# A decode kernel's five instruction streams, emitted into the program itself instead of into a Block

## Chip, cores and metric

One core of a Trainium2 chip. The metric is the device time of one execution in microseconds (us), as a median over runs; lower is better. A profile also gives the span: from the first to the last recorded instruction of the core. Measured time and span are different things.

## The reference

One decode step of a transformer layer. A normalized token `xn` goes through grouped-query attention over a cache of 65,536 positions (4 key/value heads, 32 query heads, head size 128) and, in parallel, through a small MLP mixer; both are added to `x`.

```python
def reference(A_x, A_k_cache, A_v_cache, A_wq, A_wo, B_x, B_w1, B_w2, B_w3, B_w4):
    # _A_ref: q = x @ wq; softmax(q k^T / sqrt(Dh)) v over the cache; @ wo     (cut)
    # _B_ref: layernorm, w1, gelu, shifted groups, w2, layernorm, w3, gelu, w4  (cut)
    x = A_x
    xn = _layernorm(x, axis=-1)
    return x + _A_ref(xn, A_k_cache, A_v_cache, A_wq, A_wo) + _B_ref(xn, B_w1, B_w2, B_w3, B_w4)
```

The output is one row of 1024 bfloat16 values. The caches and weights are about 170 MB, all read once.

## The kernel before

Each engine has a queue object that records waits, operations and DMAs; dependencies become waits until a semaphore, a counter that engines and DMAs raise, has reached a constant. At the end the recorded lists are emitted, one per engine, into a `Block`. A Block gives each engine a body of its own to branch to, and behind the bodies it places a meeting of all five engines, called the rendezvous here: nobody leaves until all have arrived.

```python
class _Q:
    def emit(self, eng):
        for o in self.ops:
            if o[0] == 0:
                eng.wait_ge(o[1], o[2])          # wait on a semaphore
            elif o[0] == 1:
                ins = o[1](eng)
                if o[2]:
                    ins.then_inc(self.sem, 1)
            else:
                o[1](eng).then_inc(o[2], 16)     # DMA

    with ExitStack() as es:
        E = es.enter_context
        block = E(nc.Block())                    # entered first, so left last
        # ... (cut: tiles, semaphores, the whole computation recorded into q_pe, q_dve, q_act, q_pool, q_sp)
        for i in range(len(w4_parts)):
            w4_pe(i)                             # the last matmuls, into OUT_ps
        _op(q_dve, lambda e: e.tensor_copy(orow[:, :], OUT_ps[:, 0:256]), reads=[b_OUT], writes=[b_orow])
        ev_out = _dma(q_sp, chan("out"), lambda e: e.dma_start(out=out[0, 0, :].rearrange("(j n) -> j n", j=4), in_=orow[0:97:32, :]), reads=[b_orow])
        q_sp.wait(ev_out)                        # SyncE waits until the store has landed

        block.sync(lambda e: q_sp.emit(e))
        block.tensor(lambda e: q_pe.emit(e))
        block.vector(lambda e: q_dve.emit(e))
        block.scalar(lambda e: q_act.emit(e))
        block.gpsimd(lambda e: q_pool.emit(e))
```

## Time and profile before

| | before |
|---|---|
| measured time, median of 3 runs | 403.76 us (403.68 to 404.6) |
| span in the profile | 401.93 us |
| measured time of the profiled run | 403.64 us |
| last weights land | 398.93 us |
| store issued, store landed | 399.87, 401.53 us |

A DMA lands when the last update of its semaphore is recorded. "The landing" below is that of the output's store.

The page of the kernel before says what bounds it. The lines are its span, the busy time of each engine, the load queue (packets, MB, share of the 16 DMA engines' time) and the chain that ended last, by engine.

```profile
span 401.9 us, 5169 instructions
...
PE 193.7 (48%) x2059; PEld 83.0 (21%) x2059; DVE 227.8 (57%) x400; ACT 48.3 (12%) x127; POOL 61.8 (15%) x90
...
q1 hardware_dynamic: 6920, 169.87, 98.4%
...
DMA 54%; DVE 22%; PE 17%; ACT 3%; issue 2%; SPq 0%; POOL 0%; ACTq 0%
...
```

No compute engine is near its limit, and one queue keeps the DMA engines 98.4% occupied: the kernel moves its bytes as fast as the DMA engines do. The view by windows (busy time with the number of instructions for each engine, then the TensorE clock, the DMA share and GB/s) shows where this holds and where it ends:

```profile
...
core 0: us, PE busy (x) PEld busy (x) DVE busy (x) ACT busy (x) POOL busy (x), PEclk, DMA share, GB/s
...
20.00:100.00 80.00, 34.26 (x472) 15.21 (x469) 45.77 (x92) 9.13 (x22) 8.71 (x10) 1.00 1.00 431
...
300.00:380.00 80.00, 38.83 (x324) 12.34 (x328) 55.87 (x90) 12.51 (x34) 14.40 (x16) 0.61 1.00 430
380.00:399.00 19.00, 11.05 (x194) 6.12 (x190) 1.50 (x5) 0.60 (x1) 1.09 (x1) 0.68 0.88 373
399.00:402.00 3.00, 0.36 (x8) 0.08 (x8) 0.42 (x1) 0.00 (x0) 0.00 (x0) 1.00 0.00 1
...
```

From 20 to 380 us the DMA share is 1.00. In the last three microseconds it is 0.00: the loads are over, and the kernel's own steps there follow one another: last matmuls, cast, store, end. A step removed from that sequence should shorten the kernel by its length. The end of the timeline (start, duration, engine, line, operation; a "q" behind the engine marks its sequencer) shows the sequence:

```profile
...
399.42 0.42 DVE L619 CAST orow<-OUT_ps 128x256 bf16<-128x256 f32 x1 [13.16 <-PE OUT_ps L392]
399.87 0.65 SPq L620 DMA_DIRECT2D out_dram<-orow  x1
```

After the cast and the issue of the store there is no further work, yet the span goes on to 401.93 us. The view of SyncE's waits and the view of the line that opens the Block (engine, operation, count; durations in ns; first and last start in us) show why:

```profile
...
engine line waited for: us in total, times, longest us
...
SPq L155 <- DMA out_dram<-orow: 1.0, 1, 1.0
...
SPq L155 <- PEq L155: 0.2, 1, 0.2
```

```profile
...
L155 POOLq EVENT_SEMAPHORE  x2: 17/17/17, 401.7 to 401.8; - x2
L155 ACTq DRAIN  x1: 627/627/627, 381.2 to 381.2; - x1
L155 POOLq DRAIN  x1: 1197/1197/1197, 381.8 to 381.8; - x1
L155 PEldq DRAIN  x1: 435/435/435, 399.0 to 399.0; - x1
L155 DVEq DRAIN  x1: 464/464/464, 399.4 to 399.4; - x1
L155 SPq COMPARE_BRANCH  x1: 33/33/33, 401.6 to 401.6; - x1
L155 SPq DRAIN  x1: 7/7/7, 401.7 to 401.7; - x1
L155 SPq EVENT_SEMAPHORE  x1: 17/17/17, 401.9 to 401.9; - x1
L155 ACTq EVENT_SEMAPHORE  x1: 17/17/17, 401.9 to 401.9; - x1
L155 DVEq EVENT_SEMAPHORE  x1: 21/21/21, 401.9 to 401.9; - x1
L155 PEldq EVENT_SEMAPHORE  x1: 51/51/51, 401.9 to 401.9; - x1
...
```

SyncE waits 1.0 us for the store, in its branch (the branch instruction carries the wait), and then 0.2 us in the rendezvous. Everything of L155 that starts at 401.6 us or later stands behind the landing of the store. The drains (the DRAIN instructions that the Block puts behind each stream) of the other four engines are over by 399.90 us.

### The profile page before, as it was taken

The page shows a single profiled execution, that of the slowest core. Times are in us where ns is not written, and L with a number is a line of the kernel's source. Part 1 is how long each engine was busy: PE and PEld are TensorE (multiplying, and loading weights), DVE is VectorE, ACT ScalarE, POOL GpSimd, SP SyncE. Part 2 cuts the span into 40 slices and gives each one's busy share as a digit, 9 for nine tenths or more (in the row PEclk, how much of TensorE's full clock was granted, in tenths as well). Part 3 has the DMA queues.
Part 4 walks back from the last instruction along what each step waited for, and adds up shares of the span by engine and source line. Part 5 has one row for each costly group of instructions (what it writes and reads, how often), then busy time and mean ns, then how long its engine had stood idle before and what let it go on. Part 6 is the DMA issues. An engine that isn't in the chain of part 4 may idle for free.

```text
span 401.9 us, 5169 instructions
## 1 busy us (share of the span) xinstructions
PE 193.7 (48%) x2059; PEld 83.0 (21%) x2059; DVE 227.8 (57%) x400; ACT 48.3 (12%) x127; POOL 61.8 (15%) x90
## 2 busy tenths in 40 slices
PE   0361446064525756286640965454443645445645
PEld 0250111021103511062110731121111311111232
DVE  0217666277816588255753388576836775788410
ACT  0000201012101011011110011111201111111200
POOL 5000013011211011110310102111110112112110
PEclk9999999999955565555565556565565855665686
DMA  8999999999999999999999999999999999999994
GB/s 356 427 416 436 444 421 419 450 432 421 444 434 423 432 434 439 416 434 452 423 420 450 426 424 444 432 421 435 430 435 427 445 430 424 424 431 430 436 419 205
DMA packets 7088, 170.20 MB, mean 423 GB/s; under 512 B 916, under 2 KB 920, under 8 KB 1048
## 3 DMA queue, kind: packets, MB, share of 16 engines
q1 hardware_dynamic: 6920, 169.87, 98.4%
q8 instruction: 16, 0.26, 0.2%
q14 instruction: 8, 0.07, 0.0%
q10 hardware_dynamic: 144, 0.00, 0.0%
HBM read 169.87 MB, written 0.00 MB: 423 GB/s over the span
## 4 chain that ended last, share of the span: by engine, by line
DMA 54%; DVE 22%; PE 17%; ACT 3%; issue 2%; SPq 0%; POOL 0%; ACTq 0%
DMA Kn<-in_A_k_cache_dram 43%; DVE X L464 11%; DMA Kn<-in_B_w_dram 6%; DMA Vn<-in_A_wq_dram 5%; PE H_ps L367 4%; DVE pT_f L517 3%; PE S_ps L476 3%; PE OT_ps L524 3%; DVE mrow L483 3%; ACT p_sb L506 3%; PE M_ps L367 2%; PE PT_ps L515 2%; PE M_ps L552 1%; PE OUT_ps L392 1%; DVE Yall L381 1%
## 5 line engine op out<-in xcount | busy, mean ns | idle before, releaser
L464 DVE STREAM_TRANSPOSE X<-Kn 128x1024 f32<-128x1024 f32 x128 | 151.7, 1215 | 64.2 <-DMA Kn<-in_A_k_cache_dram 64.2
L524 PE MATMUL OT_ps<-Vn,pT_f 128*32 128x512 bf16 x512 | 59.9, 620 | 27.2 <-DVE pT_f L517 27.2
L476 PE MATMUL S_ps<-X,Yall 128*32 128x512 bf16 x512 | 57.5, 593 | 17.0 <-DVE X L464 17.0
L489 PE MATMUL MB_ps<-Rm,Lmat 128*128 128x16 bf16 x32 | 6.1, 192 | 87.3 <-DVE Rm L484 87.3
L538 POOL TENSOR_TENSOR O_acc<-O_acc,tmpO 128x513 f32<-128x513 f32 x28 | 32.9, 1174 | 89.0 <-ACT tmpO L532 89.0
L506 ACT ACTIVATE p_sb<-S_ps,brun 128x512 bf16<-128x512 f32 x32 | 22.0, 687 | 172.3 <-DVE brun L504 153.8
L536 POOL TENSOR_SCALAR O_acc<-O_acc,ff 128x513 f32<-128x513 f32 x28 | 19.5, 698 | 149.8 <-ACT ff L511 149.8
L515 PE MATMUL PT_ps<-p_sb,permR 128*128 128x512 bf16 x32 | 18.2, 568 | 39.7 <-ACT p_sb L506 39.7
L483 DVE TENSOR_REDUCE mrow<-S_ps 128x1 f32<-128x512 f32 x32 | 21.6, 674 | 24.2 <-PE S_ps L476 24.2
L532 ACT ACTIVATE tmpO<-OT_ps 128x512 f32<-128x512 f32 x32 | 19.1, 598 | 107.6 <-PE OT_ps L524 107.6
L476 PEld LDWEIGHTS S_ps<-X,Yall 128*32 128x32 bf16 x512 | 16.5, 125 | 54.8 <-DVE X L464 38.6
L517 DVE STREAM_TRANSPOSE pT_f<-PT_ps 128x512 f32<-128x512 f32 x32 | 22.9, 716 | 7.6 <-PE PT_ps L515 7.6
L524 PEld LDWEIGHTS OT_ps<-Vn,pT_f 128*32 128x32 bf16 x512 | 14.5, 127 | 59.2 <-DVE pT_f L517 42.4
L489 PEld LDWEIGHTS MB_ps<-Rm,Lmat 128*128 128x128 bf16 x32 | 3.3, 102 | 111.2 <-DVE Rm L484 111.2
L367 PEld LDWEIGHTS H_ps<-xn_bf,W 128*128 128x128 bf16 x224 | 14.4, 174 | 1.7 <-issue 1.7
L367 PE MATMUL H_ps<-xn_bf,W 128*128 128x1 bf16 x224 | 14.5, 202 | 0.0
L515 PEld LDWEIGHTS PT_ps<-p_sb,permR 128*128 128x128 bf16 x32 | 3.4, 106 | 42.4 <-ACT p_sb L506 42.4
L493 DVE TENSOR_REDUCE Bst<-MB_ps 128x1 f32<-128x16 f32 x32 | 5.6, 174 | 8.3 <-PE MB_ps L489 8.3
L331 PE MATMUL M_ps<-ln_s,ones_f 128*128 128x1 f32 x6 | 1.8, 363 | 17.5 <-DVE ln_s L330 17.5
L534 POOL COPY O_acc<-tmpO 128x513 f32<-128x513 f32 x4 | 2.4, 612 | 47.6 <-ACT tmpO L532 47.6
L392 PE MATMUL OUT_ps<-Kn,gh_bf 128*1 128x256 bf16 x112 | 6.4, 402 | 5.5 <-DMA Kn<-in_B_w_dram 5.5
L619 DVE CAST orow<-OUT_ps 128x256 bf16<-128x256 f32 x1 | 0.4, 425 | 13.2 <-PE OUT_ps L392 13.2
(101 smaller groups left out, 117.3 us busy)
## 6 DMA issues: line engine op xcount, KB each, us to landing
Kn<-in_A_k_cache_dram SPq DMA_DIRECT2D x15, 4096.0 KB, 27.5
Vn<-in_A_v_cache_dram SPq DMA_DIRECT2D x15, 4096.0 KB, 22.2
W<-in_B_w_dram SPq DMA_DIRECT2D x2, 3584.0 KB, 24.9
W<-in_A_wo_dram SPq DMA_DIRECT2D x3, 2048.0 KB, 24.3
Kn<-in_A_wq_dram SPq DMA_DIRECT2D x1, 4096.0 KB, 12.2
Vn<-in_A_wq_dram SPq DMA_DIRECT2D x1, 4096.0 KB, 21.4
W<-in_B_w_dram SPq DMA_DIRECT2D x2, 2048.0 KB, 32.1
Kn<-in_A_k_cache_dram SPq DMA_DIRECT2D x2, 2048.0 KB, 24.9
```

Source lines behind the costliest of these rows:

```text
L367: fns.append(lambda e, j=j, cx=cx: e.matmul(ps_tile[:, c0 + cx:c0 + cx + 1], lhs_fn(j - j0, cx), rhs_fn(j), start=(j == 0 and cx == 0), st ...
L392: fns.append(lambda e, lhs=lhs, rhs=rhs, jj=jj: e.matmul(OUT_ps[32 * jj:32 * jj + 1, 0:256], lhs, rhs[:, 256 * jj:256 * jj + 256], start=F ...
L464: _op(q_dve, lambda e, ix=ix: e.transpose(out=X32[:, xs, 1024 * ix:1024 * (ix + 1)], in_=Kn32[:, s, 4096 * half + 1024 * ix:4096 * half + ...
L476: fns.append(lambda e, we=we, cm=cm, mv=mv: e.matmul(S_ps[32 * cm:32 * cm + 32, :], Yall[:, h, we, :, :].rearrange("p a g -> p (a g)"), mv ...
L483: _op(q_dve, lambda e: e.reduce_max(mrow[:, m:m + 1], S_ps[:, :], axis=AX.X), reads=[b_S], writes=[b_mrow[m]])
L506: _op(q_act, lambda e: e.activation(p_sb[:, m, :], S_ps[:, :], ACTF.Exp, bias=brun[:, kn:kn + 1], scale=SCALE, accum_out=tmpO[:, m, 512:513]),
L515: _op(q_pe, lambda e: e.matmul(PT_ps[:, :], permR[:, :], p_sb[:, m, :], start=True, stop=True), reads=[b_p[m], b_const], writes=[b_PT])
L517: _op(q_dve, lambda e: e.transpose(out=pT_f[:, :], in_=PT_ps[:, :]), reads=[b_PT], writes=[b_pT])
L524: fns.append(lambda e, q=q, q4=q4: e.matmul(OT_ps[32 * q4:32 * q4 + 32, :], pT_bf[:, q, :, 1], Vn[:, s, 8192 * half + 512 * q:8192 * half ...
L532: _op(q_act, lambda e: e.activation(tmpO[:, m, 0:512], OT_ps[:, :], ACTF.Copy), reads=[b_OT], writes=[b_tmpO[m]], partial=True)
L536: _op(q_pool, lambda e: e.tensor_scalar(out=O_acc[:, :], in0=O_acc[:, :], scalar1=ff[:, m:m + 1], scalar2=0.0, op0=ALU.mult, op1=ALU.add), ...
L538: _op(q_pool, lambda e: e.tensor_tensor(out=O_acc[:, :], in0=O_acc[:, :], in1=tmpO[:, m, :], op=ALU.add), reads=[b_tmpO[m]], writes=[b_Oacc])
```

## The change

The intent is to lose the Block's branches, drains and rendezvous. The recorded lists are the same; only where they are emitted changes, and SyncE's wait for the store becomes the last instruction of its stream.

```diff
     with ExitStack() as es:
         E = es.enter_context
-        block = E(nc.Block())
 ...
         q_sp.wait(ev_out)
 
-        block.sync(lambda e: q_sp.emit(e))
-        block.tensor(lambda e: q_pe.emit(e))
-        block.vector(lambda e: q_dve.emit(e))
-        block.scalar(lambda e: q_act.emit(e))
-        block.gpsimd(lambda e: q_pool.emit(e))
+        q_sp.emit(nc.sync)
+        q_act.emit(nc.scalar)
+        q_pool.emit(nc.gpsimd)
+        q_dve.emit(nc.vector)
+        q_pe.emit(nc.tensor)
```

## The prediction

> **What bounds the kernel now.** DMA bandwidth. The page of the profile gives 169.87 MB read at a mean 423 GB/s over a span of 401.9 us, with one queue keeping the 16 DMA engines 98.4% occupied. The windows view gives a DMA share of 1.00 and 430 to 432 GB/s from 20 to 380 us. No compute engine is near its limit (VectorE 57%, TensorE 48%). The chain that ended last is 54% DMA, and its end is exposed: the last piece of w4 lands at 398.93 us, eight matmuls and a 0.42 us cast follow, the store is issued at 399.87 us (0.65 us) and lands at 401.53 us.
>
> **What the change does.** The per-engine instruction lists are the same, with the same waits and DMA order; only their container changes. In the trace, everything that the container adds is at the end (the view of the source line that opens the Block): one branch on SyncE, which carries the wait for the store (401.55 us, 33 ns), five drains, and the rendezvous of all engines through GpSimd. I find no branch at the start: the first DMAs are issued at 0.79 us, right after the start-up rendezvous that ends at about 0.73 us and belongs to the program, not to the Block; it stays.
>
> What goes:
> - Drains of ScalarE (0.63 us), GpSimd (1.20), TensorE (0.44) and VectorE (0.46): all over by 399.90 us, while the store is under way until 401.53 us. Off the critical path, worth nothing.
> - SyncE after the landing: branch at 401.55, its drain at 401.71, GpSimd's two semaphore instructions at 401.75 and 401.83, the release of the engines at 401.87 to 401.93 us. On the critical path: 401.93 - 401.55 = 0.38 us.
>
> What comes: one semaphore wait on SyncE as an instruction by itself; those take 17 ns here. Net gain of the span 0.36 us, so 401.57 us. The measured time (403.76 us) holds some 1.8 us that lie outside the span. It could gain a little more if the other four engines, no longer held until 401.9 us, run ahead into whatever closes the execution. "Runtime: NRT & Kernel Launch" of the Trainium skill (section on the preamble/postamble breakdown) states that the runtime puts a barrier of its own behind the kernel, about 1.5 us; then the Block's rendezvous is doubled by another that still waits for SyncE, the last engine, and removing it gains no more than its own length. The trace shows no instructions of that closing part, so this stays unchecked.
>
> The instructions could be fetched at other places; the 16 fetches of that queue take 0.2% of the DMA time, so nothing is to be had there.
>
> **Prediction.** 403.76 - 0.4 = 403.4 us, 8 in 10 between 402.6 and 404.2 us (the three runs of before spread over 0.9 us). Faster by over 2%: 0.01; within 2%: 0.98; slower: 0.01.
>
> **What would show each step right.** (1) The span ends with SyncE's wait, within 0.1 us of the store's landing, near 401.6 us. (2) No instruction of the old Block line: late drains, branch and rendezvous gone, ten instructions or more fewer. (3) The store's issue stays at 399.9 us within 0.3 us. (4) DMA share and GB/s by stage the same. (5) Start-up rendezvous and first DMA at 0.79 us the same.
>
> **What would make it wrong.** Another placement of the activation table load (1.28 us at 44.1 us, before the first exponential); an engine waiting for instruction fetch in the new layout; a closing part that gets longer or overlaps with the store; or a DMA stream at a different rate on another chip, which would hide 0.4 us.

## The result and the profile after

| | before | after |
|---|---|---|
| measured time, median | 403.74 us (403.67 to 404.6, 6 runs) | 402.85 us (402.69 to 402.98, 6 runs) |
| ratio | | 0.9975, 95% interval 0.9962 to 0.9988 |
| span in the profile | 401.93 us | 401.59 us |
| measured time of the profiled run, less its span | 1.71 us | 1.24 us |

A ratio here is the mean time of one kernel's runs over the mean of the other's in the same rounds, so it is not quite the ratio of the two medians. By the 2% rule the two kernels are the same; by the interval the change is a gain of a quarter of a per cent.

The medians differ by 0.89 us (the two profiled runs by 0.81, 403.64 against 402.83). The span shrank by 0.34 us. So more than half of the gain lies where the profile's page shows nothing: outside the span. The page and the windows of the kernel after, to be held against those of before:

```profile
span 401.6 us, 5142 instructions
...
PE 187.7 (47%) x2043; PEld 84.2 (21%) x2059; DVE 227.8 (57%) x400; ACT 48.4 (12%) x127; POOL 62.0 (15%) x90
...
q1 hardware_dynamic: 6920, 169.87, 98.4%
...
DMA 54%; DVE 24%; PE 17%; issue 2%; ACT 2%; another core or an unknown queue 1%; SPq 0%; POOL 0%; ACTq 0%
...
```

```profile
...
core 0: us, PE busy (x) PEld busy (x) DVE busy (x) ACT busy (x) POOL busy (x), PEclk, DMA share, GB/s
...
20.00:100.00 80.00, 32.47 (x470) 15.25 (x470) 45.96 (x92) 9.33 (x23) 8.72 (x10) 1.00 1.00 431
...
300.00:380.00 80.00, 36.52 (x316) 12.09 (x324) 55.88 (x90) 12.53 (x34) 14.46 (x16) 0.59 1.00 429
380.00:399.00 19.00, 13.48 (x202) 7.60 (x202) 1.50 (x5) 0.60 (x1) 1.09 (x1) 0.59 0.88 374
399.00:402.00 3.00, 0.40 (x8) 0.00 (x0) 0.42 (x1) 0.00 (x0) 0.00 (x0) 0.50 0.00 1
...
```

The DMA share and the rates are the same within 1 GB/s until the end, and the queue moved the same bytes, so the gain doesn't come from the load stream. (PE's 2043 matmuls against 2059 are records missing from the trace; both kernels have the same matmuls.) The end of the timeline and SyncE's wait for the store:

```profile
...
399.45 0.42 DVE L618 CAST orow<-OUT_ps 128x256 bf16<-128x256 f32 x1 [11.34 <-PE OUT_ps L391]
399.90 0.65 SPq L619 DMA_DIRECT2D out_dram<-orow  x1
```

```profile
...
SPq L46 <- DMA out_dram<-orow: 1.0, 1, 1.0
...
```

The store is issued at 399.90 us (399.87 before), and SyncE again waits 1.0 us for it, now in the plain wait of the emitting loop (L46). There is no line of a Block any more. At the start nothing changed: the first load is issued at 0.79 us in both traces.

### Looking outside the span

The trace also records every update of a semaphore, with its time, and these records go on after the last instruction. One semaphore, number 2, which no line of either kernel uses, is updated nine times in quick steps near the end, and nine times more 0.8 us later. "Runtime: NRT & Kernel Launch" of the Trainium skill, section "Semaphores 0–2 are reserved", names it: it is the sync barrier of the runtime. Its section "The ~15µs preamble/postamble breakdown" describes the preamble's pass of this barrier as a serpentine across the five engines, eight hops of 44 ns, about 355 ns. Nine updates with eight gaps fit that: right before the first instruction of the kernel before the semaphore is also updated nine times, in 0.371 us, and at the end, where the other engines are not late, the first to the ninth took 0.358 us (experiment `pe_waits` below). I call the first nine the closing chain. These are its nine updates in the two profiles, worked out as time less the landing of the store:

```
us from the landing of the store
          1st     2nd     3rd     4th     5th     6th     7th     8th     9th    measured time - 9th
before  +0.637  +0.671  +0.883  +0.927  +0.950  +1.048  +1.087  +1.121  +1.168   +0.94
after   -1.973  -1.939  -1.900  -1.537  +0.150  +0.193  +0.231  +0.265  +0.312   +0.96
```

This is the finding. Before, the whole chain ran after the rendezvous, so after the landing. After, the first four steps were taken 1.97 to 1.54 us before the landing, three of them even before the store was issued (at -1.66 us); only the fifth waited for it. (The clock of the measured time does not start with the span's, so its distance from the ninth update has no meaning by itself; that it is the same does: what follows the ninth update did not change.)

### The profile page after: what moved, and what is told of

It reads as the page before. It is cut to its first block, busy times and chain, and to the rows that moved or that the text cites. A ratio compares the mean times of both kernels' runs of the same rounds, so it can differ in the third digit from the quotient of the medians.

```text
span 401.6 us, 5142 instructions
## 1 busy us (share of the span) xinstructions
PE 187.7 (47%) x2043; PEld 84.2 (21%) x2059; DVE 227.8 (57%) x400; ACT 48.4 (12%) x127; POOL 62.0 (15%) x90
## 4 chain that ended last, share of the span: by engine, by line
DMA 54%; DVE 24%; PE 17%; issue 2%; ACT 2%; another core or an unknown queue 1%; SPq 0%; POOL 0%; ACTq 0%
DMA Kn<-in_A_k_cache_dram 43%; DVE X L463 12%; DMA Kn<-in_B_w_dram 6%; DMA Vn<-in_A_wq_dram 5%; PE H_ps L366 4%; DVE pT_f L516 3%; PE S_ps L475 3%; PE OT_ps L523 3%; DVE mrow L482 3%; PE M_ps L366 2%; ACT p_sb L505 2%; PE PT_ps L514 1%; PE M_ps L551 1%; PE OUT_ps L391 1%; DVE Yall L380 1%
## 5 line engine op out<-in xcount | busy, mean ns | idle before, releaser
L514 PE MATMUL PT_ps<-p_sb,permR 128*128 128x512 bf16 x16 | 9.5, 594 | 21.2 <-ACT p_sb L505 21.2
L551 PE MATMUL M_ps<-O_acc,cb_W 128*128 128x128 f32 x32 | 7.4, 403 | 2.0 <-DVE cb_W L544 2.0
```

The lines of the kernel that those rows point to most:

```text
L514: _op(q_pe, lambda e: e.matmul(PT_ps[:, :], permR[:, :], p_sb[:, m, :], start=True, stop=True), reads=[b_p[m], b_const], writes=[b_PT])
L551: fns.append(lambda e, t=t: e.matmul(M0_ps[:, 128:256], cb_W[:, t, :, :].rearrange("p g i -> p (g i)"), O_acc[:, t * P:(t + 1) * P], start ...
```

## The experiments

Three theories were on the table when the runs began; the expectations name them by letter.

- **O, overlap.** Only what comes after the landing of the store costs time. The Block cost its own instructions there and, by holding four idle engines until then, it also pushed their share of the closing chain behind the landing.
- **B, branches.** The part outside the span was long because the Block's program ends with branches to another place.
- **L, length.** The rendezvous costs its length wherever it stands.

Every kernel below gave a correct result. All were timed for five rounds beside the kernel before, whose medians were 403.81, 403.78 and 403.85 us in the three groups (block_wait_behind, both bar runs and pe_waits; after_again, dve_waits, act_waits and all_wait; the other three). The landing itself moves by some tenths of a microsecond from run to run (401.53 to 401.92 us in the profiles), so besides the time I compare the ends by what follows the landing in each profile (one profiled run each; the last column takes the measured time of that run):

| run | median us | ratio to before, 95% interval | end of span - landing | 1st update | 3rd | 5th | 9th | measured time - landing |
|---|---|---|---|---|---|---|---|---|
| before | 403.74 | | 0.398 | +0.637 | +0.883 | +0.950 | +1.168 | 2.11 |
| after | 402.85 | 0.9975 (0.9962 to 0.9988) | 0.033 | -1.973 | -1.900 | +0.150 | +0.312 | 1.27 |
| after_again | 402.82 | 0.9974 (0.9962 to 0.9987) | 0.034 | -1.943 | -1.870 | +0.150 | +0.315 | 1.27 |
| block_wait_behind | 403.12 | 0.9984 (0.9970 to 0.9998) | 0.033 | -0.084 | +0.162 | +0.229 | +0.447 | 1.39 |
| bar_early | 403.01 | 0.9980 (0.9968 to 0.9993) | 0.033 | -0.086 | +0.160 | +0.227 | +0.445 | 1.40 |
| bar_late | 403.77 | 0.9998 (0.9986 to 1.0011) | 0.293 | +0.532 | +0.777 | +0.844 | +1.062 | 2.02 |
| dve_waits | 403.10 | 0.9982 (0.9969 to 0.9996) | 0.049 | -1.990 | -1.917 | +0.218 | +0.434 | 1.38 |
| act_waits | 403.10 | 0.9983 (0.9970 to 0.9995) | 0.038 | -1.981 | +0.190 | +0.258 | +0.476 | 1.46 |
| pe_waits | 403.21 | 0.9985 (0.9973 to 0.9998) | 0.079 | +0.271 | +0.343 | +0.411 | +0.629 | 1.58 |
| pool_waits | 403.46 | 0.9991 (0.9979 to 1.0004) | 0.040 | -1.943 | +0.578 | +0.646 | +0.864 | 1.82 |
| all_wait | 403.57 | 0.9991 (0.9979 to 1.0004) | 0.080 | +0.301 | +0.579 | +0.645 | +0.864 | 1.82 |
| block_no_drain | 403.78 | 0.9997 (0.9984 to 1.0011) | 0.479 | +0.715 | +0.959 | +1.027 | +1.246 | 2.19 |
| act_stores | 402.91 | 0.9977 (0.9965 to 0.9990) | 0.033 | -1.997 | -0.273 | +0.150 | +0.313 | 1.27 |

### block_wait_behind: the whole Block, the store's wait behind it

```diff
-        q_sp.wait(ev_out)
+        with nc.Block() as block:
-        block.sync(lambda e: q_sp.emit(e))       # and the other four
+            block.sync(lambda e: q_sp.emit(e))   # and the other four
+        nc.sync.wait_ge(*ev_out)
```

> The Block is kept with its branches, drains and rendezvous; only the wait for the store stands behind the Block. Theory O (overlap: the end costs what comes after the store's landing; the Block's rendezvous and the first four steps of the runtime's own closing rendezvous can run while the store is under way): ratio to the kernel before about 0.998, 402.8 to 403.0 us, as fast as the kernel after; the closing semaphore's last update about 0.3 us after the landing (before 1.17, after 0.31). Theory L (the Block costs its length wherever it stands): no gain, 403.6 to 403.8 us. Theory B (the branches that end the Block make the closing part slow): most of the outside gain of 0.5 us is missing, 403.3 to 403.5 us, if the branch costs also when it is taken early.

Measured: 403.12 us, a ratio of 0.9984, and the chain's ninth update 0.447 us after the landing. This is 0.69 us less than the median of before on the same chip (403.81 us), with all of the Block's branches, drains and rendezvous still in the program (building it shows two branches per engine; its trace records none), so L falls: a Block that ends while the store is under way costs 0.12 us after the landing (1.39 against 1.27 us), where it cost 0.84 us behind it. Under B, 403.3 to 403.5 us was expected if a branch costs also when it is taken early, which falls too; a branch that costs only behind the landing is left to bar_late. But O as I had put it was off: 403.12 us where 403.0 was its upper end, and not 0.31 but 0.45 us to the ninth update. The chain is not finished with its first half when the store lands, and what holds it is its third step, GpSimd's: GpSimd's last instruction ends at 401.18 us and the third update comes 0.57 us later, at +0.162 us. The fifth, SyncE's, is then 0.08 us later than in after. The other 0.06 us lie between the fifth and the sixth update (0.098 against 0.043 us); why is not traced. bar_early, below, shows the same.

### bar_late and bar_early: the same rendezvous, behind or ahead of the store's wait, no Block

```diff
 bar_late
         q_pe.emit(nc.tensor)
+        nc.all_engine_barrier()
```

```diff
 bar_early
-        q_sp.wait(ev_out)
 ...
         q_pe.emit(nc.tensor)
+        nc.all_engine_barrier()
+        nc.sync.wait_ge(*ev_out)
```

> No Block, no branches, but a rendezvous of all engines as the last thing, after the wait for the store. Theory O: nearly the time of before, less the branch that SyncE took (0.16 us between branch and drain) and the one behind it: 403.3 to 403.6 us; the closing semaphore's first update comes after the landing and its last one 0.8 to 1.0 us after it. Theory B: only the rendezvous itself (0.2 us) comes back, 402.85 + 0.2 = 403.05 us or less, and the part of the time outside the span stays at 1.24 us as in the kernel after (before 1.74 us in the profiled run).

> The same instructions as in bar_late, but the wait for the store stands behind the rendezvous. Theory O: the rendezvous ends near 400.9 us, 0.6 us before the landing, so it costs nothing: 402.8 to 402.95 us, the four first updates of the closing semaphore near 401.1 us, before the landing. Theory L: as bar_late within 0.1 us.

Measured: 403.77 us with the rendezvous behind the wait, 403.01 us with it ahead. The same instructions, in another order on SyncE alone, are 0.76 us apart. The view of the rendezvous' line in bar_late and then in bar_early, GpSimd's and SyncE's part of it:

```profile
...
L627 POOLq EVENT_SEMAPHORE  x2: 17/17/17, 402.0 to 402.1; - x2
...
L627 SPq DRAIN  x1: 13/13/13, 402.0 to 402.0; - x1
L627 SPq EVENT_SEMAPHORE  x1: 17/17/17, 402.1 to 402.1; - x1
...
```

```profile
...
L626 POOLq EVENT_SEMAPHORE  x2: 17/17/17, 401.1 to 401.2; - x2
...
L626 SPq DRAIN  x1: 417/417/417, 400.6 to 400.6; - x1
L626 SPq EVENT_SEMAPHORE  x1: 17/17/17, 401.2 to 401.2; - x1
...
```

In bar_late SyncE's drain starts at 402.0 us, after the landing at 401.92 us. In bar_early it starts at 400.6 us, right behind the issue of the store, and the rendezvous is over by 401.3 us, while the store lands at 401.60 us. SyncE then still waits for the store, in both versions that end so (bar_early first, then block_wait_behind):

```profile
...
SPq L627 <- DMA out_dram<-orow: 0.4, 1, 0.4
SPq L626 <- PEq L626: 0.2, 1, 0.2
```

```profile
...
SPq L627 <- DMA out_dram<-orow: 0.4, 1, 0.4
SPq L621 <- PEq L621: 0.2, 1, 0.2
```

bar_late has no branch at all and is as slow as before (ratio 0.9998): 403.77 us where B said 403.05 at most. That settles B for the bulk of the time. What is left between the two is the branch and whatever else the Block's form adds: measured time less landing is 2.11 us in before and 2.02 in bar_late, so about 0.09 us, from one profile each. My figure for bar_late under O was 403.3 to 403.6 us, below what was measured; in its profile the store landed late, at 401.92 us against 401.53 in before. It was issued 0.37 us later, at 400.24 us, for which this experiment has no reason to give. (The 1.74 us that the recorded text names for before is 1.71 by the unrounded span.) Counted from the landing, its ninth update at 1.062 us is just above the 0.8 to 1.0 expected. In bar_early the ninth update was expected as in after and came 0.13 us later, because the rendezvous ended later than I had worked out: SyncE's drain took 417 ns behind the issue, against 13 ns in bar_late, and GpSimd's step came another 0.57 us after its last instruction. Its time, 403.01 us, is just above the 402.95 expected.

### pe_waits: another engine as the last to arrive

```diff
-        q_sp.wait(ev_out)
+        q_pe.wait(ev_out)
```

> The kernel after, but TensorE waits for the store and not SyncE. No instruction more or less. Theory O, with TensorE as the first in the closing chain (its first update came at 399.59 us in the kernel after, 0.2 us after TensorE's last matmul): all nine updates have to come after the landing, the last about 0.5 to 0.6 us after it against 0.31, so 403.05 to 403.2 us. If only the number of instructions or the branches count (theory B): as the kernel after, 402.75 to 402.95 us.

Measured: 403.21 us, and all nine updates after the landing, the last at +0.629 us. There is not one instruction more than in the kernel after, no rendezvous and no branch, and still the end is 0.31 us longer after the landing (1.58 against 1.27 us). So the place of the last engine in the closing chain counts, as O says, and TensorE is the first in it. Not all of the 0.32 us by which the ninth update is later is its place, though: 0.12 us is TensorE's longer way to its own step (+0.271 us against SyncE's +0.150), and 0.20 us is the longer rest of the chain. Both figures lie just above what was expected (0.6 us at most for the ninth update, 403.2 us for the time).

### after_again, dve_waits, act_waits, pool_waits: the order of the chain

```diff
-        q_sp.wait(ev_out)
+        q_dve.wait(ev_out)     # dve_waits;  q_act in act_waits, q_pool in pool_waits
```

> The kernel after once more, on the chip of the next three, so that differences of 0.1 us can be read. 402.8 to 403.0 us. The closing semaphore's ninth update 0.31 us after the store's landing (0.312 in the first profile), and the measured time of the profiled run 0.95 us after that ninth update, as in all six profiles so far (0.94 to 0.96).

> VectorE waits for the store in place of SyncE. Theory O with the chain in the order that the first profiles suggest (TensorE first, VectorE fourth, SyncE fifth and turning point): the first three updates come before the landing, the fourth about 0.15 us after it, the ninth about 0.39 us after it, so 0.08 us more than the kernel after. If the four early engines were equal in the chain: as with TensorE, 0.63 us, 0.3 us more than after.

> ScalarE waits for the store. Theory O, if ScalarE is second in the chain: one update before the landing, eight after it, the ninth about 0.47 us after the landing: 0.16 us more than the kernel after, between dve_waits and the run in which TensorE waited (0.63 us). If it is third, about 0.04 us less.

> GpSimd alone waits for the store. If place in the chain were all (ninth update 0.63 us after the landing with TensorE, 0.48 with ScalarE, 0.43 with VectorE, 0.31 with SyncE), GpSimd as third would give 0.44 to 0.46 us and about 403.0 us. If GpSimd has a slow way into the closing part of its own (0.57 us from its release to the third update in the kernel before, 0.54 us in all_wait), the third update comes 0.58 us after the landing and the ninth 0.86 us, the same as when all five wait: 403.4 to 403.6 us, slower than TensorE alone though it stands later in the chain.

The repeat of after gave 402.82 us with the ninth update at +0.315 us. With VectorE waiting, three updates come before the landing and the ninth at +0.434; with ScalarE one, and the ninth at +0.476; with GpSimd two. So the chain is TensorE, ScalarE, GpSimd, VectorE, SyncE; that the other four updates are the way back fits the count, but no run tests it. Apart from GpSimd, the later the waiting engine stands in it, the less is left after the landing. The expected 0.39 and 0.47 us were met within 0.05. The times of these two runs, both 403.10 us, can't tell them apart: their five runs each spread over 0.7 to 0.8 us. What holds them apart is the chain in the profiles.

GpSimd breaks the order, as the second reading in its expectation had it: third in the chain, it is the costliest engine to leave for last. Its update comes 0.54 us after the end of its wait (its 17 ns wait starts 0.023 us after the landing, the third update comes at +0.578), where SyncE takes 0.12 and ScalarE 0.11 us. pool_waits ends at +0.864 us, the same as when all engines wait.

### all_wait: held back, but without a rendezvous

```diff
-        q_sp.wait(ev_out)
+        for q in (q_sp, q_act, q_pool, q_dve, q_pe):
+            q.wait(ev_out)
```

> All five engines wait for the store; no rendezvous, no drain, no branch. It holds the engines back as the Block's end did, without its instructions. Theory O: the whole closing chain comes after the landing, the ninth update 0.63 us after it (as when TensorE alone waits), or 0.80 if the gap of 0.21 us between second and third update, which all three kernels with a rendezvous showed against 0.04 us in the others, comes from GpSimd having been held back: 0.3 to 0.5 us more than the kernel after. If only rendezvous or branch instructions make the closing part long: as the kernel after.

Measured: 403.57 us, ninth update at +0.864. Both are above what was expected (0.80 us for the ninth update, at most 0.5 us more than the kernel after; it was 0.75 us more than after_again). This run takes the Block's cost apart. It holds every engine until the landing and has none of the Block's instructions, and counted from the landing it shows two thirds of what the Block cost (0.55 of 0.84 us). By the medians it is 0.75 of 0.96 us, and the interval of its ratio holds 1, so the times alone do not tell it from before. With the measured time less the landing of each profile as a ladder:

```
after      1.27 us
all_wait   1.82 us   +0.55   all engines held until the landing: the closing chain no longer overlaps the store (GpSimd alone held gives the same 1.82 us)
bar_late   2.02 us   +0.20   the rendezvous itself, behind the landing
before     2.11 us   +0.09   SyncE's branch, and what else the Block's form adds
```

It also answers the gap between second and third update, 0.21 us in the runs with a rendezvous and 0.04 in pe_waits: it is 0.24 us here, without a rendezvous. It is GpSimd's slow way into the closing part, seen whenever GpSimd was held.

### block_no_drain: are the drains worth anything?

```diff
-        block = E(nc.Block())
+        block = E(nc.Block(no_gpsimd_drain=True))
```

> The kernel before, with the Block's option that leaves out GpSimd's drain (1.20 us at 381.8 us). The drain lies 17 us before the end and GpSimd has nothing else to do: 403.6 to 403.9 us, ratio 1.000 within 0.0005; ninth update 1.17 us after the landing as before. If the drain is what makes GpSimd late in the closing chain (the gap of 0.21 us between second and third update), the ninth comes 0.17 us earlier: 403.6 us.

Measured: 403.78 us, ratio 0.9997. (The drain of before ends 18.9 us before the end of the span; the 17 us of the recorded text is the distance to the store's issue.) GpSimd's drain of 1.20 us, the longest of the Block's instructions, is gone and nothing is gained. The option makes each engine's arrival an instruction of its own, which on SyncE stands behind the landing: the ninth update came 0.08 us later than in before. The gap between second and third update is still 0.21 us, so the drain was not what made GpSimd late.

### act_stores: a try at a shorter store

```diff
-        ev_out = _dma(q_sp, chan("out"), ...)
+        ev_out = _dma(q_act, chan("out"), ...)
```

> The kernel after, with the store issued by ScalarE and still awaited by SyncE: an attempt at a shorter way from the cast to the landing, which all versions share (issue 0.65 us, landing 1.66 us after its start on SyncE). If ScalarE's issue takes as long, no change: 402.75 to 402.95 us. If it takes 0.40 us, as for the load of x, up to 0.25 us less: 402.6 us. The second step of the closing chain is ScalarE's and would then come after its issue, near 400.7 us, still before the landing, so the ninth stays at 0.31 us.

Measured: 402.91 us, no gain. The end of its timeline:

```profile
...
399.92 1.10 ACTq L619 DMA_DIRECT2D out_dram<-orow  x1
```

The issue on ScalarE took 1.10 us instead of 0.65, and ScalarE's step of the chain came at 401.29 us and not near 400.7. Yet the store landed 1.68 us after its start, against 1.66 in the kernel after. In both, the first packet of the store moved 1.25 to 1.26 us after the issue began, so the issuing sequencer's busy time is not on the way to the landing. "DMA: Bandwidth & Descriptors" of the Trainium skill, section "Issuing engines are not separate DMA queues", says that DMAs run on the same 16 DMA engines whichever engine starts them, and that starting them on several engines saves only time on the sequencer. One store moved to another engine is a narrower case; its unchanged landing agrees.

No version was found that beats the kernel after. Of the places for the last wait, SyncE, which the change already uses, leaves the least after the landing.

## Why the prediction was right or wrong

The predicted 403.4 us with a range of 402.6 to 404.2 held the measured 402.85, and "within 2%" was right. Neither says much of the mechanism: the range reached 0.8 us to either side, twice the predicted gain, and held the time of before too. The gain itself was 0.89 us between the medians, and the 0.36 to 0.4 us predicted are less than half of that. Point by point:

- **What bounds the kernel: right.** DMA shares and rates are the same before and after within 0.01 and 1 GB/s, and the store is issued within 0.03 us of the same time in both profiles.
- **The span: right.** Predicted 401.57 us, measured 401.59; SyncE's wait is the last instruction, ending 0.033 us after the landing. The part of the old span behind the landing, 0.398 us, shrank by 0.365; 0.36 was predicted.
- **The drains worth nothing: right**, and tested for the longest of them (block_no_drain).
- **Start and store: right.** First DMA at 0.79 us in both traces, the store's issue at 399.90 against 399.87 us. Eleven instructions fewer, once the 16 unrecorded matmuls are set aside (5169 - 5142 - 16). The built program of before does have a branch per engine at its start, which left no record; the first load comes at 0.79 us with and without it.
- **The failed step, a term mis-sized: "removing it gains no more than its own length".** It was argued from the runtime's own barrier behind the kernel: two meetings in a row, the second waits for SyncE anyway. That the barrier is there, and that it waits for SyncE, is right. What I missed is that this barrier is itself a sequence, in which four of the five engines come ahead of SyncE, and that they can take their steps before the store has landed. The Block's rendezvous forbade that. In the profiles, the distance from the landing to the chain's ninth update fell from 1.168 to 0.312 us, by 0.86 us, where 0.365 us are the Block's own; the other 0.49 us are the overlap, which all_wait takes away again without a Block (+0.55 us; the two ways of dividing the sum differ by 0.06 us). The prediction had the right thought one sentence earlier, engines that "run ahead into whatever closes the execution", called it "a little more", and argued it away.
- **What carried the mis-sizing:** the records to see it were in the trace of before. The nine updates behind the span's end, all after 402.17 us, were there to be read; I said that the trace shows no instructions of the closing part and stopped, though its semaphore records go on.

What is not settled: why GpSimd needs 0.54 us into the closing part was not traced to an instruction, since none is recorded there. The same holds for the constant 0.94 to 0.99 us between the ninth update and the measured end.

## What to carry to other kernels

What this barrier cost at the end of the kernel was less its own length (0.20 us, and 0.09 us for the Block's form) than what it kept from overlapping (0.55 us). Ask what the waiting engines would do next, even if that belongs to the runtime. If a rendezvous must stay, end it while the store is still under way and put the store's wait behind it, on SyncE; this recovered most of the gain with the Block intact (403.12 against 403.81 us). And of the five engines, GpSimd was the one not to hold until last: alone it cost as much as all five (+0.55 us). When measured time and span move by different amounts, look at the records behind the last instruction before settling on a cause.

## What the Trainium skill lacked or had wrong

- "Runtime: NRT & Kernel Launch", preamble/postamble breakdown: the postamble's barrier is one row, about 1.5 us, "wait for all engines done". It lacks that engines which are done early take their steps in it early, so that what is left of it depended here on which engine ended last. Measured from the landing of the store to its ninth update: 0.31 us with SyncE last, 0.43 VectorE, 0.48 ScalarE, 0.63 TensorE, 0.86 GpSimd or all five held.
- The same table gives 44 ns for each hop of the preamble's serpentine, 355 ns for eight. The total is near (0.371 us before the kernel's first instruction in before, 0.358 us at the end of pe_waits), but the hops were not alike: 0.023 to 0.112 us in the first, 0.024 to 0.097 us in the second. When GpSimd was held, the gap to its step was 0.21 to 0.24 us (0.04 otherwise), eight gaps 0.53 us in the kernel before. None of the pages I read has GpSimd's 0.54 us from the end of its wait to its step.
- "DMA: Bandwidth & Descriptors", anatomy of one DMA: it breaks down the path through GpSimd and gives most of about 2 us to the write receipt. Beyond a single figure for the first byte, the page has no such breakdown for a store issued by SyncE or ScalarE. The store here, issued by SyncE, took 1.66 us, of which 1.25 us passed before its first packet moved and 0.32 us between its last packet and the landing.
- None of the pages I read says that the recorded duration of an issue need not tell when the data moves: this store's issue lasted 0.65 us on SyncE and 1.10 us on ScalarE, with the first packet 1.25 to 1.26 us after its start and the same time to the landing within 0.02 us.
